# A gated mix of linear attention and a squared-ReLU layer: all products as two streams of 64-row halves, in one fixed order for all engines

## The chip, the cores and the metric

The kernel runs on one core of a Trainium2 chip. The metric is the device time of one execution in microseconds (us). The kernel before took 447.13 us, the median of three runs (446.76 to 447.21).

The engines are named as in the profile: PE (TensorE, matmuls), PEld (its weight loads), DVE (VectorE), ACT (ScalarE), POOL (GpSimd), SP (SyncE, which issues most DMAs). SBUF and the accumulators in PSUM have 128 partitions, here called rows where a matmul contracts over them. PSUM is used in eight banks of 128 x 512 float32.

## The reference

All tensors are float32; S = 2048 tokens, D = 448, F = 1792, 16 heads of 28.

```
x = A_x
g = sigmoid((x * gate_w).sum(-1))
q, k, v = split(x @ wqkv)                      # per head
phi = lambda t: where(t > 0, t + 1, exp(t)) + 1e-6
pq, pk = phi(q), phi(k)
kv = einsum("bhsd,bhse->bhde", pk, v);  z = pk.sum over s
o = (pq @ kv) / (pq . z + 1e-6)
a = o @ wo
h = relu(x @ w1 + b1) ** 2
b = h @ w2 + b2
return g * a + (1 - g) * b
```

## The kernel before

**Precision.** Each float32 operand is split into a rounded high part and the rest (`split_hi`, `split_lo`), and a product is computed as three: high times high, high times low, low times high. Over the D = 448 input columns that is 3 x 448 = 1344 rows of contraction. The host pads x and the weights to four chunks of 128 rows, the last of which holds columns 384 to 447 twice; `split_last` writes high and low parts crosswise into its two halves, so that two matmuls do the work of three there. A product over D thus takes 11 matmuls (`terms_x`, `terms_w`, `up_chunk`).

**Tiling.** Tokens go in four blocks `b` of 512, each of four tiles of 128. The squared-ReLU layer goes over F in 14 slices `f` of 128: `up(b, f)` makes `h_ps` (128 x 512, 11 matmuls), `hidden` applies bias, ReLU and square on ACT and splits the result into `hh` and `hl` on DVE, and `down(b, f)` adds its product with `w2` into the four banks `o_ps` (12 matmuls of 448 columns). The seven first slices of all blocks come first, then the seven others; `half_done` and `finish` empty `o_ps`.

**Attention** is worked in between. In the first phase `keys(t)` makes `k_ps` (11 matmuls) and phi of it, and `gram(b, c)` sums products of keys and tokens in `g_ps`. Then `key_sums` (`z_ps`), `kv_product` (`kv_ps`) and `m_product` (`m_ps`) fold v and wo into one matrix `m_s`, which POOL's DMAs put together. In the second phase `queries(b, c)` (`q_ps`; 11 matmuls, 7 for the fourth block, whose halves are swapped by DMAs and added), `denominators(b)` (`d_ps`), `scaled` and `attention(b, i)` (`a_ps`, 11 matmuls) follow.

**Order and buffers.** Two loops over `b` and `f` write the steps in the order up, down, attention work, loads and splits; work that empties a bank is put off by one step (`todo`, `run_todo`). The framework places the instructions of each engine from that. Banks come from three pools: four for `o_ps`, two for `h_ps`, two for the rest. Most SBUF buffers are 14 rotating slots of one tag (`slot`); the queries' operands are 15 of another (`late`).

Of the kernel before, what the change touches and what calls it, by code (L numbers as in the profile page):

```python
# [1 line left out]

# [12 lines left out]
DH = D // H  # L15
# [13 lines left out]

@with_exitstack  # L30
def gated_mix_kernel(ctx: ExitStack, tc: tile.TileContext, xt, xn, wk, wq, wv, wo, w1a, w1b, w2, b1, b2, hmask,
                     kvmask, halves, out):
    nc = tc.nc
    act, dve, pool, pe, sp = nc.scalar, nc.vector, nc.gpsimd, nc.tensor, nc.sync
# [10 lines left out]
    NSLOT, NLATE = 14, 15  # L45

    def slot(shape, dt, name):
        return work.tile(shape, dt, name=name, tag="s", bufs=NSLOT)
# [25 lines left out]
    def products(out_ps, terms):  # L74
        n = len(terms)
        for i, (a, b) in enumerate(terms):
            pe.matmul(out_ps, a, b, start=(i == 0), stop=(i == n - 1))  # L77


    def terms_x(xh, xl, cols, w, wcols, c):  # L80
        if c == 3:
            return [(xh[:, 3, cols], w[:, 3, wcols]), (xl[:, 3, cols], w[:, 3, wcols])]
        return [(xh[:, c, cols], w[:, c, wcols]), (xh[:, c, cols], w[:, 4 + c, wcols]),
                (xl[:, c, cols], w[:, c, wcols])]

    def terms_w(xh, xl, w, wcols):
        t = []
        for c in range(3):
            t += [(w[:, c, wcols], xh[:, c]), (w[:, c, wcols], xl[:, c]), (w[:, 4 + c, wcols], xh[:, c])]
        return t + [(w[:, 3, wcols], xh[:, 3]), (w[:, 3, wcols], xl[:, 3])]  # L90

# [5 lines left out]
    def load_x(b, c, a=0, z=TB):  # L97
        if a == 0:
            x_raw[b, c] = slot([P, TB], F, f"xr{b}_{c}")
        load(x_raw[b, c][:, a:z], xt[b, c][:, a:z])  # L100

    def split_x(b, c, a=0, z=TB):
        if c == 0 and a == 0:
            xs[b] = (keep.tile([P, 4, TB], R, name=f"xh{b}", tag="xh", bufs=2),
                     keep.tile([P, 4, TB], R, name=f"xl{b}", tag="xl", bufs=2))
        (xh, xl), r = xs[b], x_raw[b, c]
# [6 lines left out]
    def split_w(w, c, src, hi_eng, lo_eng):  # L113
        split_hi(hi_eng, w[:, c], src)
        if c < 3:
            split_lo(lo_eng, w[:, 4 + c], src, w[:, c])
        else:
            split_lo(lo_eng, w[64:, 3], src[64:], w[64:, 3])
# [4 lines left out]
    def load_w1(h, g, c):  # L123
        w1_raw[h, g, c] = slot([P, (TB, 3 * P)[g]], F, f"w1r{h}{g}{c}")
        load(w1_raw[h, g, c], (w1a, w1b)[g][h, c])

    def split_w1(h, g, c, hi_eng=act):
        if c == 0:
            w = keep.tile([P, (3648, 2716)[g]], R, name=f"w1_{h}{g}", tag=f"w1{g}", bufs=1)

            n, a = (4, 3)[g], ((4, 20), (4, 16))[g][h]
            w = w[:, a:a + 900 * n].rearrange("p (i k) -> p i k", k=900)[:, :, :7 * P]
            w1_s[h, g] = w.rearrange("p i (c j) -> p c i j", c=7)
        split_w(w1_s[h, g], c, w1_raw.pop((h, g, c)).rearrange("p (i k) -> p i k", k=P), hi_eng, dve)


    W2_AT = [56, 48, 40, 28, 20, 12, 4, 18, 14, 17, 15, 16, 2, 10]
    w2_s, w2_raw = {}, {}

    def load_w2(f):  # L140
        w2_raw[f] = slot([P, D], F, f"w2r{f}")
        load(w2_raw[f], w2[f])

    def split_w2(f):
        w = keep.tile([P, 960], R, name=f"w2_{f}", tag="w2", bufs=NH)
        w = w[:, W2_AT[f]:W2_AT[f] + 2 * D]
        w2_s[f] = w.rearrange("p (s n) -> p s n", s=2)
        split_hi(act, w2_s[f][:, 0], w2_raw[f])
        split_lo(dve, w2_s[f][:, 1], w2_raw.pop(f), w2_s[f][:, 0])
# [3 lines left out]
    def load_xn(t):  # L153
        xn_raw[t] = slot([P, D], F, f"xnr{t}")
        load(xn_raw[t], xn[t])
# [3 lines left out]
    def load_wk(c):  # L159
        wk_raw[c] = slot([P, D + 2], F, f"wkr{c}")  # L160
        load(wk_raw[c], wk[c])

    warm = keep.tile([P, 400], mybir.dt.bfloat16, name="warm")[:, :256]
    dve.memset(warm, 0.0)
# [4 lines left out]
    side = rest.tile([P, 56], F, name="side")[:, :2]  # L172
# [11 lines left out]
    b1_s = keep.tile([P, NF], F, name="b1_s")  # L184
    half = keep.tile([P, 2], F, name="half")
    ones = keep.tile([P, 2], F, name="ones")
    logit = keep.tile([P, NT], F, name="logit")
    gate = keep.tile([P, 2, NT], F, name="gate")
    zc = keep.tile([P, 4], F, name="zc")
# [14 lines left out]
    tmp_p = phase1.enter_context(tc.tile_pool(name="tmp_p", bufs=1, side="right"))  # L204

# [3 lines left out]
    def up_chunk(ps, b, f, c):  # L209
        h, fl = divmod(f, NH)  # L210
        g, i = divmod(fl, 4)
        w, cols = w1_s[h, g], i
        xh, xl = xs[b]
        if c < 3:
            terms = [(w[:, c, cols], xh[:, c]), (w[:, c, cols], xl[:, c]), (w[:, 4 + c, cols], xh[:, c])]
        else:
            terms = [(w[:, 3, cols], xh[:, 3]), (w[:, 3, cols], xl[:, 3])]
        for n, (a, m) in enumerate(terms):
            pe.matmul(ps, a, m, start=(c == 0 and n == 0), stop=(c == 3 and n == 1))  # L219

    def hidden(ps, b, f):
        r = slot([P, TB], F, f"hr{b}_{f}")
        act.activation(r, ps, AF.Relu, bias=b1_s[:, f:f + 1])  # L223
        act.activation(r, r, AF.Square)  # L224
        h = slot([P, TB], R, f"hh{b}_{f}")
        lo = slot([P, TB], R, f"hl{b}_{f}")
        split_hi(dve, h, r)
        split_lo(dve, lo, r, h)
        hs[f] = (h, lo)

    def up(b, f):
        ps = mm_p.tile([P, 512], F, name=f"h_ps{b}_{f}", tag="mm")
        for c in range(4):
            up_chunk(ps, b, f, c)
        hidden(ps, b, f)

    o_ps = {}

    def down(b, f, tiles=range(4)):
        h, lo = hs[f]  # L240
        w = w2_s[f]
        for i in tiles:
            if f % NH == 0:
                o_ps[i] = acc_p.tile([P, 512], F, name=f"o_ps{b}_{f}_{i}", tag="acc")
            cols = slice(i * P, (i + 1) * P)
            terms = [(h[:, cols], w[:, 0]), (h[:, cols], w[:, 1]), (lo[:, cols], w[:, 0])]
            for n, (a, m) in enumerate(terms):
                pe.matmul(o_ps[i][:, :D], a, m, start=(f % NH == 0 and n == 0),  # L248
                          stop=(f % NH == NH - 1 and n == 2))

    def half_done(b):
        for i in range(4):
            dve.tensor_tensor(part[4 * b + i], o_ps[i][:, :D], b2_s, op=ALU.add)

    def finish(b, i):
        t = 4 * b + i
        u = slot([P, D], F, f"out{t}")
        dve.scalar_tensor_tensor(u, o_ps[i][:, :D], gate[:, 1, t:t + 1], part[t], op0=ALU.mult, op1=ALU.add)
        sp.dma_start(out=out[t * P:(t + 1) * P, :], in_=u)
# [3 lines left out]
    gsum = []  # L263
# [5 lines left out]

    def keys(t):  # L270
        b, i = divmod(t, 4)
        ps = ms_p.tile([P, 512], F, name=f"k_ps{t}", tag="ms")
        products(ps[:, :D + 2], [term for c in range(4)
                                 for term in terms_x(*xs[b], slice(i * P, (i + 1) * P), wk_s, slice(0, D + 2), c)])
        e = slot([P, D], F, f"e{t}")
        r = slot([P, D], F, f"r{t}")
        p = r
        ph = tmp_p.tile([P, D], R, name=f"ph{t}", tag="ph", bufs=4)
        pl = tmp_p.tile([P, D], R, name=f"pl{t}", tag="pl", bufs=4)

        if t == 0:
            pool.memset(tmp_p.tile([P, 48], F, name="off"), 0.0)

        def after():
            phi(ps[:, :D], e, r, p)
            dve.tensor_copy(logit[:, t:t + 1], ps[:, D:D + 1])
            split_hi(act, ph, p)
            split_lo(dve, pl, p, ph)
            if t == 0:
                pool.tensor_copy(ksum, p)  # L290
            else:
                pool.tensor_tensor(ksum, ksum, p, op=ALU.add)  # L292
            nh = tmp.tile([P, 512], R, name=f"nh{t}", tag="nh", bufs=4)
            nl = tmp.tile([P, 384], R, name=f"nl{t}", tag="nl", bufs=4)
            raw = xn_raw.pop(t)
            split_hi(act, nh[:, :D], raw)
            split_lo(pool, nl, raw[:, :384], nh[:, :384])
            split_lo(pool, nh[:, D:], raw[:, 384:], nh[:, 384:D])
            pend[t] = (ph, pl, nh, nl)
        return [after]  # L300

    def gram(b, c):
        ps = ms_p.tile([P, 512], F, name=f"g_ps{b}_{c}", tag="ms")
# [5 lines left out]
        products(ps[:, :D], terms)  # L309

        def after():
            if b == 0:
                gsum.append(tmp.tile([P, D], F, name=f"gsum{c}"))
                act.copy(gsum[c], ps[:, :D])
            else:
                dve.tensor_tensor(gsum[c], ps[:, :D], gsum[c], op=ALU.add)
        return [after]

    wq_s = keep.tile([P, 7, TB], R, name="wq_s")
# [438 lines left out]
```

## Time and profile before

| | |
|---|---|
| median of 3 runs | 447.13 us |
| the profiled execution: span from first to last instruction | 445.7 us |
| matmuls in the program / in the trace | 2034 / 2054 |
| DMA: moved, mean rate | 28.77 MB, 65 GB/s |

The program's 20 float32 matmuls (`kv_ps`, `z_ps`) stand in the trace as two each, hence 2054. A matmul row gives the time from its start to the modelled end of its result, so successive rows overlap; the pace of the matmuls is the difference of their starts, or the length of a group divided by its count. Idle time stands in front of the instruction that had to wait, with what ended it.

```profile
DMA packets 18315, 28.77 MB, mean 65 GB/s; under 512 B 2880, under 2 KB 12784, under 8 KB 18288
```

### The profile page before, as it was taken

To read this page: it belongs to the slowest core of one execution; us is meant where nothing else is said; L and a number is where in the kernel's file an instruction comes from. 1 tells how busy PE (TensorE), PEld (TensorE's weight loads), DVE (VectorE), ACT (ScalarE), POOL (GpSimd) and SP (SyncE) were. 2 spreads that over 40 slices of the span, in tenths; PEclk is the share of its full clock that TensorE was granted. 3 is DMA by queue.
4 is the path that set the end of the run, shared out by engine and by line. 5 is a ranking of instruction groups with operands and counts; after the bars stand their busy time and mean duration, and the time that the engine had idled before them with its cause. 6 is when DMAs were issued, how large, how long until landed. Compare 5 with 4: busy or idle time off the path is not lost.

```text
span 445.7 us, 5473 instructions
## 1 busy us (share of the span) xinstructions
PE 438.7 (98%) x2054; PEld 381.9 (86%) x2054; DVE 269.1 (60%) x452; ACT 172.2 (39%) x298; POOL 58.0 (13%) x76
## 2 busy tenths in 40 slices
PE   8999999999999999999999989999999999999996
PEld 6798898889888888888988868888888898888885
DVE  5867536552587426672466678788455974549423
ACT  5855335331355113542344235245232443234221
POOL 0143123210252005420002420000000000000000
PEclk9999999999999999999999999999999999999999
DMA  8462202020131201332245310050100501002002
GB/s 268 149 201 68 88 0 69 24 65 22 47 116 31 66 21 43 91 100 63 71 124 146 71 38 24 1 171 6 26 0 0 179 0 26 0 0 84 1 1 82
DMA packets 18315, 28.77 MB, mean 65 GB/s; under 512 B 2880, under 2 KB 12784, under 8 KB 18288
## 3 DMA queue, kind: packets, MB, share of 16 engines
q1 hardware_dynamic: 17072, 26.81, 19.6%
q0 software_dynamic: 1216, 1.61, 1.7%
q8 instruction: 16, 0.26, 0.3%
q14 instruction: 11, 0.09, 0.1%
HBM read 22.09 MB, written 3.67 MB: 58 GB/s over the span
## 4 chain that ended last, share of the span: by engine, by line
PE 93%; DVE 3%; ACT 2%; issue 1%; DMA 1%; SPq 0%; DVEq 0%; ACTq 0%
PE h_ps L219 30%; PE o_ps L248 30%; PE q_ps L77 8%; PE a_ps L77 8%; PE g_ps L77 8%; PE k_ps L77 7%; DMA xr<-in_xt 1%; PE kv_ps L370 1%; ACT hr L223 1%; PE m_ps L77 1%; ACT hr L224 0%; DVE r L268 0%; DVE r L267 0%; PE d_ps L77 0%; DVE hh L62 0%
## 5 line engine op out<-in xcount | busy, mean ns | idle before, releaser
L219 PE MATMUL h_ps<-xh,w 128*128 128x512 f32 x392 | 128.8, 397 | 0.3 <-ACT xh L58 0.2
L248 PE MATMUL o_ps<-w,hh 128*128 128x448 f32 x448 | 126.9, 366 | 0.5 <-DVE hh L62 0.5
L248 PEld LDWEIGHTS o_ps<-w,hh 128*128 128x128 f32 x448 | 84.1, 188 | 10.8 <-DVE hh L62 1.2
L219 PE MATMUL h_ps<-xl,w 128*128 128x512 f32 x224 | 88.4, 395 | 0.0
L219 PEld LDWEIGHTS h_ps<-xh,w 128*128 128x128 f32 x392 | 73.9, 189 | 16.9 <-ACT xh L58 0.7
L248 PE MATMUL o_ps<-w,hl 128*128 128x448 f32 x224 | 80.1, 365 | 0.0
L223 ACT ACTIVATE hr<-h_ps,b_s 128x512 f32<-128x512 f32 x56 | 38.3, 683 | 102.9 <-PE h_ps L219 101.6
L62 DVE CAST hh<-hr 128x512 fp32r<-128x512 f32 x56 | 25.4, 454 | 43.6 <-ACT hr L224 43.2
L219 PEld LDWEIGHTS h_ps<-xl,w 128*128 128x128 f32 x224 | 42.4, 189 | 8.8
L248 PEld LDWEIGHTS o_ps<-w,hl 128*128 128x128 f32 x224 | 42.3, 189 | 3.6 <-DVE hl L65 0.2
L65 DVE TENSOR_TENSOR hl<-hr,hh 128x512 fp32r<-128x512 f32 x56 | 41.9, 748 | 1.9
L224 ACT ACTIVATE hr<-hr 128x512 f32<-128x512 f32 x56 | 35.3, 630 | 1.3
L77 PE MATMUL k_ps<-wk_s,xh 128*128 128x450 f32 x112 | 33.6, 367 | 0.0
L77 PE MATMUL q_ps<-xh,wq_s 128*128 128x512 f32 x100 | 33.2, 391 | 0.0
L77 PE MATMUL a_ps<-m_s,qh 128*128 128x448 f32 x112 | 32.7, 366 | 0.0
L65 POOL TENSOR_TENSOR nl<-xnr,nh 128x384 fp32r<-128x384 f32 x16 | 17.2, 1078 | 96.5 <-ACT nh L58 96.5
L487 DVE SCALAR_TENSOR_TENSOR part<-part,gate,u 128x448 f32<-128x448 f32 x16 | 10.9, 684 | 26.7 <-ACT u L486 26.7
L292 POOL TENSOR_TENSOR ksum<-ksum,r 128x448 f32<-128x448 f32 x15 | 19.3, 1284 | 52.3 <-DVE r L268 52.3
L486 ACT ACTIVATE u<-a_ps,gate 128x448 f32<-128x448 f32 x16 | 10.2, 635 | 38.1 <-PE a_ps L77 38.1
L267 DVE TENSOR_SCALAR r<-k_ps 128x448 f32<-128x448 f32 x16 | 10.0, 624 | 23.7 <-ACT e L266 23.6
L77 PE MATMUL g_ps<-pl,nh 128*128 128x448 f32 x64 | 23.3, 365 | 0.3 <-DVE pl L65 0.3
L77 PE MATMUL q_ps<-xl,wq_s 128*128 128x512 f32 x60 | 23.6, 393 | 0.0
(104 smaller groups left out, 562.5 us busy)
## 6 DMA issues: line engine op xcount, KB each, us to landing
xr<-in_xt SPq DMA_DIRECT2D x27, 256.0 KB, 3.1
xnr<-in_xn SPq DMA_DIRECT2D x16, 224.0 KB, 2.5
out<-out SPq DMA_DIRECT2D x16, 224.0 KB, 2.0
w2r<-in_w SPq DMA_DIRECT2D x14, 224.0 KB, 2.5
w1r<-in_w1a SPq DMA_DIRECT2D x8, 256.0 KB, 2.8
w1r<-in_w1b SPq DMA_DIRECT2D x8, 192.0 KB, 3.4
m_s<-m POOLq DMA_DIRECT2D x12, 112.0 KB, 2.8
wqr<-in_wq SPq DMA_DIRECT2D x4, 256.0 KB, 2.8
```

The lines of the kernel that those rows point to most:

```text
L62: eng.tensor_copy(hi, src)
L65: eng.tensor_tensor(lo, src, f32(hi), op=ALU.subtract)
L77: pe.matmul(out_ps, a, b, start=(i == 0), stop=(i == n - 1))
L219: pe.matmul(ps, a, m, start=(c == 0 and n == 0), stop=(c == 3 and n == 1))
L223: act.activation(r, ps, AF.Relu, bias=b1_s[:, f:f + 1])
L224: act.activation(r, r, AF.Square)
L248: pe.matmul(o_ps[i][:, :D], a, m, start=(f % NH == 0 and n == 0), stop=(f % NH == NH - 1 and n == 2))
L267: dve.tensor_scalar(r, ps, 0.0, 1e-6, op0=ALU.max, op1=ALU.add)
L292: pool.tensor_tensor(ksum, ksum, p, op=ALU.add)
L370: pe.matmul(kv_ps[:JE, js], wv_s[c][:, js], gsum[c][:, js], start=(c == 0), stop=(c == 3))
L486: act.activation(u, ps[:, :D], AF.Copy, scale=gate[:, 0, t:t + 1])
L487: dve.scalar_tensor_tensor(part[t], part[t], gate[:, 1, t:t + 1], u, op0=ALU.mult, op1=ALU.add)
```

## The change

**Halves.** Every matmul over 128 rows becomes two over 64: one on rows 0 to 63 (`LO`), one on rows 64 to 127 (`UP`), each with all its output columns into a whole bank. The last chunk needs no crossing trick any more: one half holds one term, the other half two, so a product over D is 21 halves instead of 11 matmuls of 128 rows. Only the last 12 matmuls of the program and the 18 warm-up ones stay whole. The program has 3938 matmuls instead of 2034.

```diff
+LO, UP = slice(0, 64), slice(64, P)
...
+def halves(terms):
+    return [[(a[r], m[r], None) for a, m in terms] for r in (LO, UP)]
+
+
+def last_halves(terms, swapped=False):
+
+    low, high = halves(terms)
+    return (low[:1], high[::-1]) if swapped else (low, high[1:])
```

**Two streams and a bank that is passed on.** The `LO` halves form one stream, the `UP` halves another. At a time a bank belongs to one of them; when its halves are done, the other stream takes the bank, and its first matmul there waits for the last one of the former stream.

```diff
+    def emit(self, j, s):
...
+        a, m, where = j.left[s].pop(0)
+        if b.of not in (None, s):
+            wait = tc.keep_in_program_order(pe.nop())
+            tc.add_manual_dep(wait.ins, b.last, AFTER, reason="the bank goes to the other half of the rows")
+        b.seen += 1 + j.whole
+        ins = pe.matmul(b.ps[where or b.whole], real(a), real(m), start=b.seen == 1 + j.whole, stop=b.seen == b.total)
+        tc.keep_in_program_order(ins)
```

In the built program the waiting no-op is merged into the matmul behind it: 322 matmuls wait for an earlier matmul, where 21 did before.

**One list.** `Flow.run` plays the whole program through with a table of durations and writes the instructions of all engines in the order that comes out (`keep_in_program_order`); each stream may choose among the next 12 products the one that can start first, and each engine among the next 60 queued operations.

```diff
+    def product(self, s):
+
+        if self.current[s] is not None:
+            return self.stream[s], self.current[s]
+        best = None
+        jobs, at = self.jobs, self.at
+        for k in range(at[s], min(at[s] + AHEAD, len(jobs[s]))):
+            j = jobs[s][k][1]
...
+            r = self.ready(j, s)
+            if r is not None and (best is None or r < best[0] - 1e-9):
+                best = r, j
...
     for b in range(1, NB):
         for f in range(NH):
+            jobs = up(b, f)
+            jobs += down(b, f - 1) if f else down(b - 1, NH - 1)
...
+    steps.append(Step(down(order[-1], NF - 1, whole=True)))
+    flow.run(steps, {"acc": 4, "mm": 2, "ms": 2})
```

**Fixed slots and layout.** Buffers are fixed tiles that an operation takes when it is written (15 slots, 14 for the queries' operands, two for `m`). The host orders the heads so that the swap of the fourth query block exchanges rows 0 to 63 with 64 to 127 in two DMAs instead of eight per block; `m_s` is put together by 32 DMAs of POOL instead of 20. `finish` adds the attention part first or last, whichever is ready later.

```diff
-            for p in range(0, P, 16):
-                load(r[p:p + 16], v[p ^ 16:(p ^ 16) + 16])
...
+            for p in (0, 64):
+                load(r[p:p + 64], v[p ^ 64:(p ^ 64) + 64])
...
-    head = 4 * (p // 32) + p % 16 // 4
...
+    head = p % 64 // 4
```

**The order on TensorE, at three places.** In the middle of block 3 (`h_ps3_2` is the product of its slice 2, `o_ps3_0_1` the bank of its second tile, `hh` and `hl` or the slots their operands, `k_ps` the keys) the program before had, one product after the other:

```order
L219 MATMUL h_ps3_2_1639<-xl3_1322,w1_00_169 128x512
L248 MATMUL o_ps3_0_0_1591<-w2_1_248,hh3_1_1587 128x448 [waits DVE_49]
L248 MATMUL o_ps3_0_0_1591<-w2_1_248,hh3_1_1587 128x448
L248 MATMUL o_ps3_0_0_1591<-w2_1_248,hl3_1_1588 128x448 [waits DVE_49]
L248 MATMUL o_ps3_0_1_1595<-w2_1_248,hh3_1_1587 128x448 x2
L248 MATMUL o_ps3_0_1_1595<-w2_1_248,hl3_1_1588 128x448
L248 MATMUL o_ps3_0_2_1599<-w2_1_248,hh3_1_1587 128x448 x2
L248 MATMUL o_ps3_0_2_1599<-w2_1_248,hl3_1_1588 128x448
```

Now the same work stands like this; the rows are halves, `LO` and `UP` in turn:

```order
L310 MATMUL o_ps3_0_0_2478<-w2_all_82,slot12_2444 128x448 [waits DVE_49]
L310 MATMUL h_ps3_1_2419<-x2_78,w10_80 128x512
L310 MATMUL o_ps3_0_1_2490<-w2_all_82,slot13_2430 128x448
L310 MATMUL h_ps3_1_2419<-x2_78,w10_80 128x512
L310 MATMUL o_ps3_0_1_2490<-w2_all_82,slot13_2430 128x448
L310 MATMUL o_ps3_0_1_2490<-w2_all_82,slot12_2444 128x448
L310 MATMUL o_ps3_0_0_2478<-w2_all_82,slot13_2430 128x448 [waits PE_49]
L310 MATMUL o_ps3_0_2_2499<-w2_all_82,slot13_2430 128x448
L310 MATMUL o_ps3_0_0_2478<-w2_all_82,slot13_2430 128x448
L310 MATMUL o_ps3_0_2_2499<-w2_all_82,slot13_2430 128x448
L310 MATMUL o_ps3_0_0_2478<-w2_all_82,slot12_2444 128x448
L310 MATMUL o_ps3_0_2_2499<-w2_all_82,slot12_2444 128x448
```

While `LO` works on the third tile, `UP` takes over the first, six halves after `LO` left it; `[waits PE_49]` marks the handover.

At the start, behind the first four `h_ps` products, the program before went on with `down(0, 0)`:

```order
L219 MATMUL h_ps0_3_164<-xl0_166,w1_00_169 128x512
L248 MATMUL o_ps0_0_0_280<-w2_0_245,hh0_0_234 128x448 [waits DVE_49]
L248 MATMUL o_ps0_0_0_280<-w2_0_245,hh0_0_234 128x448
L248 MATMUL o_ps0_0_1_284<-w2_0_245,hh0_0_234 128x448 x2
L248 MATMUL o_ps0_0_0_280<-w2_0_245,hl0_0_235 128x448 [waits DVE_49]
```

Now the first keys stand there:

```order
L310 MATMUL h_ps0_1_210<-x0_76,w10_80 128x512
L310 MATMUL k_ps0_351<-wkm_83,x0_76 128x450 [waits Activation_49]
L310 MATMUL k_ps0_351<-wkm_83,x0_76 128x450 [waits DVE_49]
L310 MATMUL k_ps0_351<-wkm_83,x1_77 128x450
L310 MATMUL k_ps0_351<-wkm_83,x0_76 128x450
L310 MATMUL k_ps0_351<-wkm_83,x0_76 128x450 [waits DVE_49]
L310 MATMUL k_ps0_351<-wkm_83,x1_77 128x450
```

The keys moved ahead of the first `down`; these halves are all of one stream, and the second stream's keys follow behind them.

In the second phase, at the denominators of block 2, the program before had:

```order
L248 MATMUL o_ps1_7_3_3114<-w2_13_2252,hl1_13_3416 128x448
L77 MATMUL d_ps2_3496<-dh2_3449,hm_135 128x512 [waits Activation_49]
L77 MATMUL d_ps2_3496<-dl2_3450,hm_135 128x512 [waits DVE_49]
L219 MATMUL h_ps2_8_3506<-xh2_3143,w1_10_1814 128x512
L219 MATMUL h_ps2_8_3506<-xl2_3144,w1_10_1814 128x512
```

and now (`x1` and `x0` hold the high and low parts of x):

```order
L310 MATMUL h_ps2_8_5531<-x1_77,w10_80 128x512
L310 MATMUL h_ps2_9_5547<-x1_77,w10_80 128x512 x2
L310 MATMUL h_ps2_9_5547<-x0_76,w10_80 128x512
L310 MATMUL h_ps2_9_5547<-x1_77,w10_80 128x512
L310 MATMUL h_ps2_9_5547<-x0_76,w10_80 128x512
L310 MATMUL h_ps2_9_5547<-x1_77,w10_80 128x512
L310 MATMUL d_ps2_5577<-slot0_5558,hm_105 128x512 [waits Activation_49]
L310 MATMUL h_ps2_8_5531<-x1_77,w10_80 128x512 [waits PE_49]
```

Six halves of `h_ps2_9` stand behind one another in the `UP` stream, with none of `LO` between them: this is one of the runs of three or more halves of one stream. There are five such runs of `LO`, with 33 halves, and seven of `UP`, with 30; all other halves alternate singly or in twos. Each stream has 916.6 thousand columns in all.

More of the change, by code (lines that the diff above doesn't have):

```diff
@@ L72, in split_last @@
         split_lo(dve, crossed, src, straight)
[L74 to L90, printed above, removed]
+    steps = []
     x_raw, xs = {}, {}
@@ L227, in hidden, with up_bank @@
         split_hi(dve, h, r)
         split_lo(dve, lo, r, h)
-        hs[f] = (h, lo)
-    def up(b, f):
[L232 to L241, printed above, removed]
+        close(r)
+        hs[b, f] = (h, lo)
+    ups, o_ps, a_banks = {}, {}, {}
+    def up_bank(b, f, pool=mm_p, tag="mm"):
+        bank = ups[b, f] = Bank(pool, f"h_ps{b}_{f}", tag, 21)
+        bank.done = lambda: hidden(bank.ps, b, f)
+        return bank
@@ L245, in down @@
[L245 to L255, printed above, removed]
-        t = 4 * b + i
-        u = slot([P, D], F, f"out{t}")
-        dve.scalar_tensor_tensor(u, o_ps[i][:, :D], gate[:, 1, t:t + 1], part[t], op0=ALU.mult, op1=ALU.add)
-        sp.dma_start(out=out[t * P:(t + 1) * P, :], in_=u)
+                o_ps[i] = Bank(acc_p, f"o_ps{b}_{f}_{i}", "acc", 6 * NH, D)
@@ new lines, in down, with half_done, store @@
+                o_ps[i].done = partial(half_done if f < NH else finish, b, i, o_ps[i])
+            terms = partial(down_terms, b, f, i)
+            split = (lambda t=terms: [[(*x, None) for x in t()], []]) if whole else (lambda t=terms: halves(t()))
+            jobs.append(Job(o_ps[i], split, C448, [("h", b, f), ("w2", f)], whole=whole))
+        return jobs
+    def half_done(b, i, bank):
+        dve.tensor_tensor(part[4 * b + i], bank.ps[:, :D], b2_s, op=ALU.add)
+    def store(t, ps, old):
+        u = slot(D)
+        dve.scalar_tensor_tensor(u, ps, gate[:, 1, t:t + 1], old, op0=ALU.mult, op1=ALU.add)
+        sp.dma_start(out=out[t * P:(t + 1) * P, :], in_=u)
+        close(u)
```

1087 lines of the change are left out of this document (704 added, 383 removed).

## The prediction

> **What bounds the kernel now.** I begin with the head of the profile page.
>
> ```profile
> span 445.7 us, 5473 instructions
> PE 438.7 (98%) x2054; PEld 381.9 (86%) x2054; DVE 269.1 (60%) x452; ACT 172.2 (39%) x298; POOL 58.0 (13%) x76
> PEclk9999999999999999999999999999999999999999
> PE 93%; DVE 3%; ACT 2%; issue 1%; DMA 1%; SPq 0%; DVEq 0%; ACTq 0%
> ```
>
> TensorE has a matmul under way in 98% of the span, its granted clock is full in all 40 slices, and 93% of the chain that ended last is TensorE. Time can only come from fewer or faster matmuls, or from the moments at which TensorE stands. I read the pace of the matmuls from the chain of waits in order of time (start, duration, piece).
>
> ```profile
> 5.31 9.89 PE h_ps L219 x38
> ...
> 166.34 2.43 PE o_ps L248 x12
> 168.77 2.25 PE k_ps L77 x11
> 171.02 2.56 PE h_ps L219 x11
> ...
> 183.27 2.27 PE k_ps L77 x11
> ...
> 205.12 2.41 PE g_ps L77 x12
> 207.53 0.79 PE z_ps L349 x8
> ...
> 223.97 3.15 PE kv_ps L370 x32
> ...
> 232.16 2.52 PE q_ps L77 x11
> ...
> 319.16 2.26 PE a_ps L77 x11
> ...
> 436.99 5.16 PE o_ps L248 x24
> 442.18 0.68 DVE out L258
> ```
>
> One matmul takes 2.56/11 = 232.7 ns in `h_ps`, 229.1 in `q_ps` (both 512 columns), 2.43/12 = 202.5 in `o_ps`, 200.8 in `g_ps`, 204.5 in `k_ps`, 205.5 in `a_ps` (448 or 450 columns). The code has 616 `h_ps`, 160 `q_ps`, 672 `o_ps`, 176 each of `g_ps`, `k_ps` and `a_ps`, and 20 of `m_ps` and `d_ps`. At these paces they take 143.3 + 36.7 + 136.1 + 35.3 + 36.0 + 36.2 + 4.3 us; with 0.79 for `z_ps` and 3.15 for `kv_ps` that is **431.8 us**. TensorE worked from 5.31 to about 442.18, which is 436.9 us: **5.1 us** were lost to waiting or to slower pieces. What it waited for is in the view of TensorE's waits (total us, times, longest):
>
> ```profile
> PE d_ps L77 <- ACT dh L58: 1.3, 1, 1.3
> PE o_ps L248 <- DVE hh L62: 0.5, 1, 0.5
> PE g_ps L77 <- DVE pl L65: 0.3, 1, 0.3
> PE h_ps L219 <- ACT xh L58: 0.2, 1, 0.2
> ```
>
> So the named waits are few, 2.3 us in all. The rest of the 5.1 us is at the start, where 38 matmuls took 9.89 us for 38 x 0.2327 = 8.84, and in small gaps.
>
> **The change, part by part.** (1) *Fewer columns through the array.* A product over 448 input columns, three terms of the precision split each, has 3 x 448 = 1344 rows of contraction, 10.5 times 128. Before, it is 11 matmuls, the last of them padded by crossing. Afterwards it is 21 halves of 64 rows, two streams of which are meant to run side by side: 10.5 pairs. If a pair takes as long as one full matmul does now, each such product saves half a matmul: 56 `h_ps` x 0.5 x 232.7 = 6.5 us, 12 of the `q_ps` x 0.5 x 229.1 = 1.4, 16 `k_ps` x 0.5 x 204.5 = 1.6, 16 `a_ps` x 0.5 x 205.5 = 1.6. `o_ps`, `g_ps`, `m_ps`, `d_ps` and four `q_ps` have no padding and save nothing. **Sum: 11.2 us off, 420.6 us of TensorE work.**
>
> (2) *The pace of a pair.* No row of this profile has two matmuls on different rows at once, so I bound it. What the trace does show is this (timeline, two stretches; PEld is the weight load):
>
> ```profile
> 208.15 0.19 PEld L219 LDWEIGHTS h_ps<-xh,w 128*128 128x128 f32 x1
> 208.26 0.19 PEld L219 LDWEIGHTS h_ps<-xl,w 128*128 128x128 f32 x1
> ...
> 300.25 0.39 PE L219 MATMUL h_ps<-xl,w 128*128 128x512 f32 x1
> 300.25 0.19 PEld L219 LDWEIGHTS h_ps<-xh,w 128*128 128x128 f32 x1
> 300.48 0.40 PE L219 MATMUL h_ps<-xh,w 128*128 128x512 f32 x1
> ```
>
> Each load starts with the matmul before it and is hidden by it. Two loads can follow each other in 208.26 - 208.15 = 0.11 us, which is half of the 0.23 us between the matmuls. From above, then: if nothing overlaps, a pair costs two matmuls; if only the loads of the two streams stand in one line, a pair costs at least 2 x 0.11 = 220 ns. That is still under the 229 to 233 ns of the 512-column pairs but 17 ns above the 203 ns of the 448-column ones. From below: the paces of the 448-column groups differ by 205.5 - 200.8 = 5 ns among themselves, and I allow 3 ns of gain on each of some 1190 such pairs, 3.6 us. I take **no change of pace**: the nearest row is the full matmul, whose columns, weight columns and clock are those of each half. Break-even stands at 11.2 us / 1960 pairs = 5.7 ns per pair, so this value decides nearly everything.
>
> The Trainium skill speaks against the change at one place: "TensorE: Matmul & The Clock Gate", section "Measured speedup vs the span model", adds about 4 ns for each further tile that runs in the array. By that, 1960 pairs would take 7.8 us more and the sum below would be 445.6 us. No run here shows it; I leave it out because a stream that follows on without a gap should not pay a start more than once.
>
> (3) *Handing a bank over.* Each bank is begun by one stream and finished by the other, so 322 matmuls now carry a wait for an earlier matmul, where 21 did. Behind such a wait stands everything in TensorE's queue, the other stream included. The nearest rows are the `k_ps` groups at 168.77 (no such wait) and 183.27 (the first of its matmuls waits for an earlier matmul): 2.25 and 2.27 us, so a wait whose cause lies a dozen matmuls back costs at most 0.02 us. In the order shown above the cause lies six or seven halves back. A bound from above: a matmul of 448 columns lives longer than its pace, and a wait that exposes the difference costs 366 - 203 = 163 ns, 52 us in all.
>
> ```profile
> L248 PE MATMUL o_ps<-w,hh 128*128 128x448 f32 x448 | 126.9, 366 | 0.5 <-DVE hh L62 0.5
> L404 POOL DMA_DIRECT2D m_s<-m x12 | 6.4, 542 | 2.2 <-DVE m L65 2.1 <-issue 0.2
> ```
>
> I take 0, by the `k_ps` rows. Break-even lies at about 30 ns per handover.
>
> (4) *Halves that run alone.* The order holds runs of three or more halves of one stream: 33 of the lower rows in five runs, 30 of the upper rows in seven. One of each run belongs to the alternation, so the other stream is idle beside (33 - 5) or (30 - 7) halves, about 25 x 0.21 = 5.3 us. These take the place of the waits of before (5.1 us); I add 1.0 us for moments at which both stand, since the start waits for the splits of x and w1, as it does now. Term: 5.3 + 1.0 - 5.1 = **+1.2 us**. Bounds: 0 to 12 us in place of the 6.3, the upper end if each run's cause is as late again.
>
> (5) *The rest I cost at nothing, with its cover.* VectorE and ScalarE do nearly the same work in another order. Their fullest stretch is in this table (us, length, then busy time and count of PE, PEld, DVE, ACT, POOL):
>
> ```profile
> 234.00:270.00 36.00, 34.66 (x156) 29.00 (x156) 25.27 (x43) 13.68 (x25) 10.57 (x20) 1.00 0.34 81
> 270.00:300.00 30.00, 30.00 (x141) 26.21 (x140) 24.02 (x40) 11.74 (x20) 0.00 (x0) 1.00 0.19 62
> ```
>
> VectorE is at 80% there, so it stays under a TensorE that is 2.6% shorter; without that cover a late `hh` costs what it costs now, 0.5 us a time. The 12 more DMAs that POOL issues for `m_s` take 12 x 0.542 = 6.5 us on a POOL that is busy 10.6 of 36 us there; they land before `a_ps` needs them as long as queries fill TensorE, otherwise up to 6.5 us appear once. The swap of the fourth query block issues 2 DMAs in place of 8, off the path. The tail (the last 12 matmuls on all rows, `out`, its DMA) is the same: 445.7 - 442.18 = 3.5 us.
>
> **The sum.** Against the profiled execution: 445.7 - 11.2 + 1.2 = 435.7 us of span. The median of the runs is 447.13, 1.4 us above the span, so the time is 437.1; the bounds of (4) lean upwards, and I say **437.8 us**, 2.1% faster.
>
> **The rivals.** *Weight loads in one line.* If both streams' loads share one path, every 448-column pair takes 220 ns: 1190 x 17 ns = 20 us, so 437.8 + 20 = **458 us**, slower. It decides from 5.7 ns per pair on. For it: two loads never stand closer than 0.11 us in this profile. Against it: here all loads use all rows, so nothing shows that loads on different rows must queue. The skill has both sides: "TensorE: Matmul & The Clock Gate", section "LDWEIGHTS (loading the stationary operand)", says that a load takes its time by columns whatever the rows, 107 ns for 128, and the trace's 0.11 us agrees; "TensorEngine Tiling (Array Packing)", section "Key Properties", says that different tiles load and multiply in parallel, which no run here shows.
>
> *Handovers that show.* If each of the 322 waits costs 40 ns (a quarter of the 163), 13 us come back: **451 us**; at 20 to 30 ns the result is 444 to 447. For it: the queue is in order, so a wait of one stream stops both. Against: the `k_ps` rows.
>
> *No overlap at all.* The change would not do what it says: 2 x 420.6 plus 16 is about **857 us**. Against it speaks only that rows that are not shared need not wait for each other.
>
> *Better than the sum.* Pairs 3 ns faster, or no halves alone: **432 us** or less.
>
> **Chances.** Forecast 0.66 (432.5 to 443), handovers or other partial loss 0.14 (443 to 452), loads in one line 0.12, no overlap 0.02, better 0.06. The range 432.5 to 452 holds the first two, 0.80, and reaches from the better end of the unknown pace to a handover of 40 ns. A measurement of this kernel can tell about 0.2% (0.9 us) from no change. Of the partial losses I put 0.05 below 446.2, 0.03 within 0.2% and 0.06 above: faster 0.66 + 0.06 + 0.05 = 0.77, same 0.03, slower 0.06 + 0.12 + 0.02 = 0.20.
>
> **What would show it.** Right: 21 halves of an `h_ps` paired with others at 230 to 235 ns per pair, `o_ps` pairs at 200 to 206, two matmuls of about 0.37 to 0.40 us starting at nearly the same time; weight loads of both streams overlapping; few waits of TensorE on itself. Wrong on (2): `o_ps` pairs at 215 to 225 ns while `h_ps` pairs keep 232. Wrong on (3): gaps of TensorE in front of halves that wait for a matmul. Wrong on (4): long waits for VectorE or ScalarE with one stream silent, above all before 20 us and between 215 and 270 us.

## The result, and the profile after

| | before | after |
|---|---|---|
| median of the runs | 446.98 us (446.76 to 447.21, 4 runs) | 441.45 us (440.80 to 443.03, 4 runs) |
| the profiled execution: its time, its span | 447.13, 445.7 us | 441.48, 439.7 us |
| start of the first to end of the last matmul of the products | 5.31 to 442.14 us | 5.38 to 436.07 us |

The ratio is **0.988** (95% interval 0.986 to 0.990): 1.2% faster, where 2.1% was forecast. The head of the page of the changed kernel (span; busy time, share and count by engine; clock by slices; the chain that ended last, by engine) answers to the one shown first in the prediction.

```profile
span 439.7 us, 9349 instructions
PE 433.8 (99%) x3978; PEld 413.3 (94%) x3978; DVE 268.5 (61%) x454; ACT 172.2 (39%) x298; POOL 67.5 (15%) x91
PEclk9999999999999999999999999999999999999999
PE 91%; DVE 5%; ACT 1%; DMA 1%; issue 0%; SPq 0%; DVEq 0%; ACTq 0%
```

Nearly twice as many matmuls fill a shorter span at the same clock. The timeline of the middle of the program (start, duration, piece; PEld is the weight load) shows that the two streams do run beside each other. At 299 us both streams multiply 512 columns:

```profile
299.29 0.39 PE L310 MATMUL h_ps<-x,w 64*128 64x512 f32 x1
299.30 0.18 PEld L310 LDWEIGHTS h_ps<-x,w 64*128 64x128 f32 x1
299.31 0.39 PE L310 MATMUL q_ps<-x,wq_s 64*128 64x512 f32 x1
299.31 0.18 PEld L310 LDWEIGHTS q_ps<-x,wq_s 64*128 64x128 f32 x1
299.53 0.39 PE L310 MATMUL h_ps<-x,w 64*128 64x512 f32 x1
...
299.54 0.39 PE L310 MATMUL q_ps<-x,wq_s 64*128 64x512 f32 x1
```

Each stream starts a half every 0.23 to 0.24 us, the pace of a whole matmul before, and the loads start 0.01 us apart. Before, two loads of 128 weight columns never stood closer than 0.108 us (those of `kv_ps`, with 112 columns, 0.10 us, so the prediction's 0.11 is not quite the least). At 189 us both work on 448 or 450 columns:

```profile
189.01 0.36 PE L310 MATMUL k_ps<-wkm,x 64*128 64x450 f32 x1
189.08 0.36 PE L310 MATMUL o_ps<-w_all,slot 64*128 64x448 f32 x1
189.21 0.36 PE L310 MATMUL k_ps<-wkm,x 64*128 64x450 f32 x1
189.28 0.36 PE L310 MATMUL o_ps<-w_all,slot 64*128 64x448 f32 x1
```

Here the step is 0.20 us in each stream. Over the whole trace, the median time from one half to the next of the same stream is 232 ns in `h_ps`, 200 in `o_ps` and 205 in `k_ps`; before, from one matmul to the next, it was 232, 203 and 205 ns. In `o_ps` the steps fall into two groups, near 200 and near 206 ns, and their mean without the gaps is 202 ns now and 203.4 before.

**What was lost.** TensorE's waits behind the warm-up (total us, times, longest) are now misleading:

```profile
PE o_ps L310 <- DVE slot L209: 0.4, 1, 0.4
PE h_ps L310 <- ACT x L209: 0.3, 1, 0.3
PE d_ps L310 <- DVE slot L209: 0.2, 1, 0.2
```

0.9 us in all, less than the 2.3 before. But such a view sees TensorE idle only when both streams stand; a stream that stands beside a busy one leaves PE busy. So I took from the trace, for each stream, the time from every matmul's start to the next one's, less a fixed pace (231.7 ns for 512 columns, 204.5 for 450, 203.5 for 448). What is left over is called **lost** below. By these paces the work is 432.7 us with 11 matmuls (or 22 halves) per product over `D`, and 421.5 us with 21 halves. Before lost 4.15 us; after lost 9.1 us in the lower stream and 9.2 in the upper. Lost is a net figure: steps that are shorter than the fixed pace are set off against the standing.

The loss is in a few places. In the table by stretches (start and end, length, then busy time and count of PE, PEld, DVE, ACT, POOL; PEclk, DMA share, GB/s), the count of matmuls tells it, not the busy time:

```profile
16.00:19.00 3.00, 3.00 (x16) 2.42 (x14) 1.32 (x3) 3.00 (x6) 0.00 (x0) 1.00 0.65 232
60.00:63.00 3.00, 3.00 (x33) 2.92 (x31) 0.81 (x2) 0.00 (x0) 0.00 (x0) 1.00 0.52 164
191.20:194.20 3.00, 2.94 (x21) 2.07 (x20) 2.60 (x5) 2.24 (x4) 1.64 (x2) 1.00 0.00 1
300.00:303.00 3.00, 3.00 (x30) 2.84 (x28) 3.00 (x5) 1.32 (x2) 0.00 (x0) 1.00 0.00 0
```

The count holds every half that is under way in the stretch. Two full streams show 30 to 33 in 3 us; from 16 to 19 us there are 16, from 191.2 on 21, with PE "busy" for all or nearly all of it. The timeline of the start, TensorE alone (start, duration, piece):

```profile
13.61 3.15 PE L310 MATMUL h_ps<-x,w 64*128 64x512 f32 x19
16.58 3.65 PE L310 MATMUL k_ps<-wkm,x 64*128 64x450 f32 x20
```

And one row of the same timeline at 191 us:

```profile
191.25 2.98 PE L310 MATMUL h_ps<-x,w 64*128 64x512 f32 x15
```

From 15.3 us on the lower stream waits, 1.0 us longer than a step, for ScalarE before its first `k_ps` half; then the upper stream, which holds no bank and finds none free, stands 2.5 us until the lower one is through with `k_ps` and hands the bank over. From 192.0 us on the same: the upper stream stands 1.5 us while the lower one runs its halves of `h_ps3_5` alone. The next largest is at 276.8 us (1.0 us), ahead of the first `a_ps`, whose first half waits for VectorE; the chain of waits there is VectorE's own work:

```profile
265.30 7.39 DVE slot L209 x12
272.69 2.47 DVE q L209 x4
...
276.37 1.61 DVE slot L209 x3
278.02 0.47 PE a_ps L310
```

The rest is in pieces of at most 0.7 us, the largest of them at 342 and 396 us.

### The profile page after: what moved, and what is told of

It reads as the page before. It is cut to its first block, busy times and chain, and to the rows that moved or that the text cites. A ratio compares the mean times of both kernels' runs of the same rounds, so it can differ in the third digit from the quotient of the medians.

```text
span 439.7 us, 9349 instructions
## 1 busy us (share of the span) xinstructions
PE 433.8 (99%) x3978; PEld 413.3 (94%) x3978; DVE 268.5 (61%) x454; ACT 172.2 (39%) x298; POOL 67.5 (15%) x91
## 4 chain that ended last, share of the span: by engine, by line
PE 91%; DVE 5%; ACT 1%; DMA 1%; issue 0%; SPq 0%; DVEq 0%; ACTq 0%
PE h_ps L310 31%; PE o_ps L310 28%; PE a_ps L310 8%; PE g_ps L310 8%; PE k_ps L310 7%; PE q_ps L310 7%; DVE slot L209 4%; ACT slot L209 1%; PE kv_ps L310 1%; DMA slot<-in_xt 1%; DVE q L209 1%; PE m_ps L310 1%; PE d_ps L310 0%; ACT x L209 0%; PE z_ps L310 0%
## 5 line engine op out<-in xcount | busy, mean ns | idle before, releaser
L310 PE MATMUL h_ps<-x,w 64*128 64x512 f32 x1176 | 257.3, 394 | 0.4 <-ACT x L209 0.3
L310 PE MATMUL o_ps<-w_all,slot 64*128 64x448 f32 (+1 forms) x1332 | 240.5, 363 | 0.4 <-DVE slot L209 0.4
L310 PEld LDWEIGHTS o_ps<-w_all,slot 64*128 64x128 f32 (+1 forms) x1332 | 205.7, 184 | 6.5 <-DVE slot L209 1.8
L310 PEld LDWEIGHTS h_ps<-x,w 64*128 64x128 f32 x1176 | 193.6, 185 | 7.5 <-ACT x L209 0.8
L310 PE MATMUL q_ps<-x,wq_s 64*128 64x512 f32 x308 | 74.3, 393 | 0.0
L310 PE MATMUL k_ps<-wkm,x 64*128 64x450 f32 x336 | 66.3, 364 | 0.0
L209 DVE TENSOR_TENSOR slot<-slot,slot 128x512 fp32r<-128x512 f32 (+2 forms) x85 | 61.3, 733 | 4.4 <-DMA slot<-slot 1.7
L310 PE MATMUL a_ps<-wkm,q 64*128 64x448 f32 x336 | 62.2, 361 | 0.1
L310 PEld LDWEIGHTS k_ps<-wkm,x 64*128 64x128 f32 x336 | 57.0, 185 | 1.4 <-ACT slot L209 0.2
L310 PEld LDWEIGHTS q_ps<-x,wq_s 64*128 64x128 f32 x308 | 55.1, 184 | 1.5 <-DVE slot L209 0.3
## 6 DMA issues: line engine op xcount, KB each, us to landing
slot<-in_w1b SPq DMA_DIRECT2D x8, 192.0 KB, 4.0
```

Source lines behind the costliest of these rows:

```text
L209: op = Op(lambda: method(*[real(x) for x in args], **{k: real(x) for k, x in kwargs.items()}), self.cost(name, kind, out, [x for x in aps ...
L310: ins = pe.matmul(b.ps[where or b.whole], real(a), real(m), start=b.seen == 1 + j.whole, stop=b.seen == b.total)
```

## The experiments

Each edit is shown against the changed kernel. "First to last" is from the first to the last matmul of the products, "lost" is as above (the mean of both streams), and the span is that of the profiled execution. Each ratio is to runs of the kernel before that were measured beside it (medians 446.98 for after, 447.15 for e1, e2, e4 and e5, 446.94 for e3, e6 and e7).

| kernel | median us | ratio to before, 95% | span | first to last | lost |
|---|---|---|---|---|---|
| before | 446.98 | | 445.7 | 436.8 | 4.2 |
| after | 441.45 | 0.988 (0.986 to 0.990) | 439.7 | 430.7 | 9.2 |
| e1_one_stream | 443.42 | 0.991 (0.990 to 0.993) | 441.7 | 432.4 | -0.3 |
| e2_22_halves | 453.07 | 1.014 (1.012 to 1.016) | 451.0 | 441.9 | 9.2 |
| e4_no_margin | 464.63 | 1.040 (1.038 to 1.041) | 462.8 | 453.3 | 31.8 |
| e5_ahead_20 | 438.09 | 0.980 (0.978 to 0.982) | 436.3 | 427.4 | 5.9 |
| e3_ahead_10 | 449.56 | 1.006 (1.004 to 1.008) | 451.1 | 442.0 | 20.4 |
| e6_one_pool | 435.74 | 0.974 (0.971 to 0.977) | 434.2 | 425.1 | 3.5 |
| e7_one_stream_ahead_6 | 449.02 | 1.004 (1.002 to 1.006) | 447.5 | 438.5 | 5.8 |

**e1: the list without the halves.** Whole matmuls over all 128 rows in one stream, with the new list, slots and layout; the padding of before (11 matmuls) is back, its low-times-low term too.

```diff
-        self.whole, self.left, self.taken, self.ready = whole, None, [False, False], [None, None]
+        self.whole, self.left, self.taken, self.ready = whole, None, [False, True], [None, None]
...
-    return [[(a[r], m[r], None) for a, m in terms] for r in (LO, UP)]
+    return [[(a, m, None) for a, m in terms], []]
...
-    return (low[:1], high[::-1]) if swapped else (low, high[1:])
+    return low, high
...
+        self.jobs[1] = []
...
-        bank = ups[b, f] = Bank(pool, f"h_ps{b}_{f}", tag, 21)
+        bank = ups[b, f] = Bank(pool, f"h_ps{b}_{f}", tag, 11)
```

> The new list, slots and layout with whole 128-row matmuls in one stream: 11 per product again, no bank is passed on. Theory idle (a pair of halves costs what one full matmul costs; what is missing from the 11.2 us is time in which one stream has nothing to do): TensorE works 11.2 us more than in the changed kernel, and the one stream is idle only some 4 us instead of 9, so about 446 to 447.5 us, the same as before; the list alone gains nothing. Rival handover (the missing 5 us are paid at waits for the other stream's matmuls): without handovers the new list would show a better order by itself, 442 us or less. Rival order (the gain came from the order and the slots, not from the halves): 441 to 442 us.

Measured: 443.42 us, faster than the theory said by some 3 us, and 1.4 us short of the two rivals, to which it is nearer. I had taken the list for neutral; alone it is worth 3.7 us against the kernel before, measured beside it (447.15). That is two thirds of the 5.5 us that the whole change gains. Four neighbouring pieces of its chain of waits (start, duration, piece):

```profile
84.31 2.24 PE k_ps L310 x11
86.55 2.50 PE h_ps L310 x11
89.05 2.43 PE o_ps L310 x12
91.48 2.41 PE g_ps L310 x12
```

Piece follows on piece without a gap, and `k_ps`, `h_ps` and `o_ps` together take 7.17 us where the prediction's rows at 166 us have 7.24. Its named waits of TensorE behind the warm-up are two (total us, times, longest):

```profile
PE h_ps L310 <- ACT x L209: 1.0, 1, 1.0
PE o_ps L310 <- DVE slot L209: 0.9, 1, 0.9
```

With them, the whole still loses nothing against the fixed paces (-0.3 us), because two things cancel. Steps that come late by more than 0.03 us add up to 2.0 us here and to 4.8 before; and the other steps are shorter, by some 1.6 us on balance (`a_ps` 200.1 ns in place of 204.0, `o_ps` 201.8 in place of 203.4, means without the gaps). The changed kernel has the shorter steps too (`a_ps` 200.9 to 201.7, `o_ps` 202.0 to 202.2), so they belong to the list or its layout and not to the halves. The halves alone, with the list already there, bring only 443.42 - 441.45 = 2.0 us (1.8 if each is compared with the kernel before measured beside it): 11.2 us of columns saved, against 9.2 + 0.3 = 9.5 us that one stream does not lose.

**e2: the padding back.** Two streams as in the changed kernel, but 22 halves per product, which adds the half that holds only low times low.

```diff
-    return (low[:1], high[::-1]) if swapped else (low, high[1:])
+    return (low, high[::-1]) if swapped else (low, high)
...
-        bank = ups[b, f] = Bank(pool, f"h_ps{b}_{f}", tag, 21)
+        bank = ups[b, f] = Bank(pool, f"h_ps{b}_{f}", tag, 22)
```

(and 22 for 21 in the banks of `k_ps`, `q_ps` and `a_ps`.)

> Two streams as in the changed kernel, but each product over D keeps its 22nd half (a low-times-low term that the changed kernel leaves out; it changes the sums only in the last bits), so the padding of before is back. Theory idle: 100 more halves, 50 pairs, that is 42 x 232 ns (h_ps, q_ps... 56 + 12 products of 512 columns and 32 of 448) = 68 x 0.5 x 0.232 + 32 x 0.5 x 0.204 = 11.2 us more: 452 to 453 us, slower than the kernel before, since the idle of two streams stays. Rival handover: also 452 to 453. Rival pace (halves of a pair slow each other): the difference to the changed kernel would be more than 11.2 us, 12 or more.

Measured: 453.07 us, 11.6 us above the changed kernel, with the same loss of 9.2 us; from the first to the last matmul the difference is 441.9 - 430.7 = 11.2 us. The saving of half a matmul per product is real and has the size of step (1). It also shows that two streams with all of the old work would be 6 us slower than before.

**e4: no margin at handovers.** The list plans a handover 0.4 us after the other stream's last half; now 0.

```diff
-LATE, SIGNAL, LANDING, HANDED = 0.25, 0.08, 1.9, 0.4
+LATE, SIGNAL, LANDING, HANDED = 0.25, 0.08, 1.9, 0.0
```

> The list is made as if a bank could be passed on at once (HANDED 0 in place of 0.4): 72 handovers have their cause only three halves back instead of 3. Its own plan leaves each stream idle about 5 us longer than that of the changed kernel. Theory idle, with a handover that costs only when its cause is nearer than about 0.4 us: 446 us by the plan, plus some 0.15 to 0.25 us for each of the about 80 close ones (both streams stop), 12 to 20 us: 458 to 466 us. Rival handover (each of the handovers costs alike, some 10 to 15 ns, whatever the distance): about 446 us.

Measured: 464.63 us, as expected by the view that a handover costs something only where its cause is near. The timeline at one of them, in which the upper half of `o_ps` takes over a bank whose last lower half started at 105.33 us, three halves back:

```profile
105.53 0.36 PE L310 MATMUL g_ps<-p,nh 64*128 64x448 f32 x1
105.75 0.47 PE L310 MATMUL o_ps<-w_all,slot 64*128 64x448 f32 x1
105.75 0.47 PE L310 MATMUL g_ps<-p,nh 64*128 64x448 f32 x1
106.06 0.36 PE L310 MATMUL o_ps<-w_all,slot 64*128 64x448 f32 x1
106.06 0.36 PE L310 MATMUL g_ps<-p,nl 64*128 64x448 f32 x1
```

The upper stream's half before had started at 105.21 us, so this one comes 0.33 us late, and the next start follows after 0.31 us in place of 0.20, in both streams. A wait for another engine acts in the same way. At 95.00 us the `o_ps` half waits for VectorE (in brackets the idle time before and what ended it); the `k_ps` half behind it in the queue waits for nothing and was due at 94.56:

```profile
94.15 0.35 PE L310 MATMUL o_ps<-w_all,slot 64*128 64x448 f32 x1
94.35 0.37 PE L310 MATMUL k_ps<-wkm,x 64*128 64x450 f32 x1
95.00 0.47 PE L310 MATMUL o_ps<-w_all,slot 64*128 64x448 f32 x1 [0.28 <-DVE slot L209]
95.00 0.47 PE L310 MATMUL k_ps<-wkm,x 64*128 64x450 f32 x1
```

A half that waits at the head of the queue thus holds the other stream as well. In this kernel the 71 handovers whose cause lies 3 halves back (a few in the changed kernel) start 0.10 us late on average. In the changed kernel those with a cause 7 to 9 halves back, the largest group (101 of 310), start within 0.004 us of the pace. Not all of the 23 us are handovers: the edit changes the list elsewhere (its plan stands 5 us longer), and for 6.8 us TensorE's granted clock was half (PEclk, the third figure from the end), which is worth at most 3.4 us:

```profile
24.80:31.60 6.80, 5.28 (x22) 4.02 (x24) 6.71 (x13) 3.33 (x7) 1.11 (x3) 0.50 0.01 4
```

What it settles is that the 0.4 us of margin buys step (3). In the changed kernel only two handovers cost much, those at 16 and 192 us (2.5 and 1.5 us in the upper stream); their causes lie two halves and one half back, since the upper stream had nothing else to start.

**e3, e5, e6: the loss itself.** If the 9 us stand because a stream finds no product to start or no free bank, then a shorter choice must lose more, and a longer one with more banks to choose from less. `AHEAD` is the number of products among which a stream chooses (12), and `PATIENCE` is by how many us the operations that come in with a step stand back in rank. e3:

```diff
-AHEAD, PATIENCE, SPARE = 12, 5.0, 3
+AHEAD, PATIENCE, SPARE = 10, 5.0, 3
```

> The changed kernel with a choice among the next 10 products for each stream instead of 12; same halves, 487 handovers instead of 474. Theory idle: the work is the same 421.5 us, the list's own plan leaves each stream idle 6.8 us longer than that of the changed kernel, so 447 to 449 us, no longer faster than the kernel before. Rival (the list's order and slots gain of themselves, one stream or two, and the halves give the rest): a slightly shorter choice changes little, 441 to 443 us.

e5, in which the second keys also take their bank from the other pool:

```diff
-AHEAD, PATIENCE, SPARE = 12, 5.0, 3
+AHEAD, PATIENCE, SPARE = 20, 9.0, 3
...
-        bank = key_banks[t] = Bank(ms_p, f"k_ps{t}", "ms", 21, D + 2)
+        bank = key_banks[t] = Bank(*((mm_p, f"k_ps{t}", "mm") if t == 1 else (ms_p, f"k_ps{t}", "ms")), 21, D + 2)
```

> Same work, same halves and about as many handovers (461 in place of 474); each stream may choose among 20 products in place of 12, steps enter with another patience (9 in place of 5), and the second keys take a bank of the h_ps pool, so that the upper rows need not wait at the start. Its own plan leaves each stream idle 4.4 us less than that of the changed kernel (5.6 in place of 10.0). Theory idle: 4.4 us faster than the changed kernel, 436 to 438 us. Rival handover: no change, 441 us.

e6, in which the two pools of two banks are one pool of four (every `"ms"` becomes `"mm"`):

```diff
-AHEAD, PATIENCE, SPARE = 12, 5.0, 3
+AHEAD, PATIENCE, SPARE = 24, 7.0, 3
...
-    mm_p = ctx.enter_context(tc.tile_pool(name="mm_p", bufs=2, space=PSUM))
-    ms_p = ctx.enter_context(tc.tile_pool(name="ms_p", bufs=2, space=PSUM))
+    mm_p = ctx.enter_context(tc.tile_pool(name="mm_p", bufs=4, space=PSUM))
+    ms_p = mm_p
...
-    flow.run(steps, {"acc": 4, "mm": 2, "ms": 2})
+    flow.run(steps, {"acc": 4, "mm": 4})
```

> The four banks of the h_ps and of the other products become one pool, so that a stream that has to wait for the other's bank can open any free one; choice among 24 products, patience 7. Same work and halves. Theory idle: the plan leaves each stream idle 5.9 us less than that of the changed kernel and 1.4 us less than the version with a choice among 20, so 435.5 to 437.5 us. Rival (below some 437 us something else ends last, the data for the start or VectorE between 240 and 280 us): no better than the version with 20, 438 us.

Measured: 449.56 and 438.09 (both just above what was expected) and **435.74 us**, with 20.4, 5.9 and 3.5 us lost. The profiled execution of e3 took 452.96 us: for 6.8 us, from 358.4 us on, its granted clock was half, behind a stretch in which the streams stood; that is up to 3.4 of its 20.4 us. All its other runs have a mean clock of 0.991 to 0.996 too, so up to some 2 us of its median are the clock. In after, e5 and e6 the clock is full between 8 us and the last matmul. The work and the halves are the same in all four kernels; from after to e6, the loss falls by 5.6 us and the time by 5.7. e6 is faster than both kernels of the case. Its table by stretches, at two of the places shown above:

```profile
16.00:19.00 3.00, 3.00 (x26) 2.66 (x26) 1.12 (x2) 2.80 (x6) 0.00 (x0) 1.00 0.97 356
...
191.20:194.20 3.00, 3.00 (x31) 2.95 (x29) 3.00 (x5) 2.17 (x4) 1.55 (x1) 1.00 0.78 229
```

and its timeline of the start, TensorE alone:

```profile
13.80 2.69 PE L310 MATMUL h_ps<-x,w 64*128 64x512 f32 x15
16.30 4.94 PE L310 MATMUL k_ps<-wkm,x 64*128 64x450 f32 x42
```

26 halves instead of 16, and 31 instead of 21: at the start the two streams now run the halves of two different `k_ps` banks, 42 in 4.9 us, and neither has to wait for the other's bank. How much of e6 is the one pool and how much the longer choice and the other patience was not tried apart.

**e7: the choice with one stream.** The edits of e1, and a choice of 6 instead of 12. Is it two streams that need the choice, or any list of this kind?

```diff
-AHEAD, PATIENCE, SPARE = 12, 5.0, 3
+AHEAD, PATIENCE, SPARE = 6, 5.0, 3
```

> One stream of whole matmuls in the new list, but with a choice among the next 6 products instead of 12. Theory: two streams need a longer choice than one, because a product occupies its bank until both streams are through; with one stream the plan grows by only 5.5 us from 12 to 6 (it grows by 19 us with two), so 447 to 449 us. Rival (the length of the choice matters alike for both): 455 us or more.

Measured: 449.02 us, 5.6 above e1. Seven of the twelve runs have a mean clock of 0.996 (in the profiled one it is half for 3.4 us, worth up to 1.7); the five at full clock took 447.65 to 448.27 us, as the theory said, 4.2 to 4.9 above e1. The view of waits names most of it (total us, times, longest):

```profile
PE o_ps L310 <- DVE slot L209: 4.1, 5, 1.1
```

One stream pays for a short choice too, but it lost nothing at 12, where two streams lost 9.2 us. With whole matmuls the wait is visible in this view; with two streams 9 us stand behind three rows of 0.9 in all.

## Why the prediction was right, and where it was not

(1) **Fewer columns**: right. Forecast -11.2 us; by the paces used here 432.7 - 421.5 = 11.2, and putting the padding back costs 11.6 (e2).

(2) **The pace of a pair**: right. The marks were 230 to 235 ns for `h_ps` and 200 to 206 for `o_ps`; measured 232, and 200 in the median and 202 in the mean. "Weight loads in one line" and "no overlap" fall with the loads 0.01 us apart. The Trainium skill's rule in "TensorE: Matmul & The Clock Gate", section "Measured speedup vs the span model", of some 4 ns for each further tile, shows only between two halves that start together, which lie 2 to 5 ns apart in the trace (19.139 and 19.143 us); it does not add to the pace, since streams that follow on keep that of one matmul. The Trainium skill's page "TensorEngine Tiling (Array Packing)", section "Key Properties", by which different tiles load and multiply in parallel, agrees with this trace.

(3) **Handovers**: right that they cost about nothing here, but the row behind the zero could not show it. The `k_ps` group at 183.27 us waits for a matmul 58 matmuls back, not a dozen, so it says nothing of a cause six or seven halves back; as far as the zero rests on that row, it came true by luck. That such handovers are free is shown by the trace after; e4 brings the causes nearer, and then they cost.

(4) **Halves that run alone**: the term that was mis-sized. I forecast 6.3 us lost in place of the 5.1 of before, +1.2. By one measure for both kernels it is 9.2 in place of 4.15, **+5.0**. The sum then reads -11.2 + 5.0 = -6.2 us, and the trace has 436.8 - 430.7 = 6.1 from the first to the last matmul; the medians differ by 5.5, since the time outside the span also grew, from 447.13 - 445.7 = 1.4 to 441.48 - 439.7 = 1.8 us.

What was mis-sized is not what the step counted. Beside the five runs of the lower rows the upper stream came 4.75 us late, beside the seven runs of the upper rows the lower stream 3.2 us: 4.0 us on average, where 5.3 was forecast. (An order does not show how long a stream stands beside a run: the twelve lower halves from 16.6 us on cost 2.5 us because the other stream had no bank, and three of the twelve runs cost nothing.) The remaining 5.2 us (net of shorter steps) stand where the step allowed 1.0, "for moments at which both stand". Sorted by what the late half itself waits for in the program, steps late by more than 0.03 us add up as follows:

| the late half waits for | lower stream, us | upper stream, us |
|---|---|---|
| a matmul of the other stream | 0.7 | 4.9 |
| VectorE or ScalarE | 5.3 | 1.3 |
| nothing | 4.2 | 4.0 |

Of the last row 0.4 and 0.8 us fall before 7 us, where the granted clock is not yet full. The others stand in the queue behind a half of the other stream that waits (0.5 us at 342.3), or follow a stop, after which the next start comes about 0.1 us late (0.31 in place of 0.20 us, as in e4). The prediction's sign for this, long waits for VectorE or ScalarE, came true, but not only at the places named ("above all before 20 us and between 215 and 270 us"): before 20 us the two streams lost 2.2 and 3.7 us, but 192 us, 276.8 us and everything behind 340 us, some 4 us in the lower stream, were not foreseen.

The bounds of that step, 0 to 12 us, did hold the value. What they hid is that two effects cancel in it: by e1 the list alone makes up for the old loss of 4.15 (less standing and shorter steps) and gains 3.7 us, and the two streams bring in a new one that is 9.5 above e1's. The step had both effects, 5.1 us off and 6.3 on, and it was the second that it made too small. The prediction weighed the list and the halves as one, and so could not see that the halves by themselves gain 2 us.

(5) **The rest at nothing**: the tail is the same (436.07 to the end of the span is 3.6 us, 3.5 before). The last rows of the timeline show the closing matmuls on all rows and the issues of the output:

```profile
434.71 1.36 PE L310 MATMUL o_ps<-w_all,slot 128*128 128x448 f32 x6
...
435.02 2.14 SPq L209 DMA_DIRECT2D out<-slot  x4
```

POOL's additional DMAs stay hidden: the last one for `m_s` is issued at 253 us, none takes over 4.0 us to land, and the first `a_ps` half at 278 us waits for VectorE alone, whose row of 7.39 us is shown above. The cover of VectorE and ScalarE did not hold as forecast: late halves that wait for them cost the lower stream 5.3 us, against 3.4 us for TensorE before by the same count. This belongs to the term of step (4).

One thing stays open: why the pieces of e1, and of all kernels with the list, are up to some 1% (in `a_ps` 2%) shorter than the same matmuls of before. No run separates the new layout from the new order.

A further remark on where the loss sits: `Flow.run` plays the program through with fixed durations before anything runs. By its own arithmetic, which is no measurement, 428.3 us pass between the starts of the first and the last product matmul of the changed kernel, with some 8 us of standing in each stream; on the chip it is 430.3 us (5.38 to 435.7). Most of the standing is planned into the list, which is why a few settings of the planner move it.

## What to carry to other kernels

Two streams of 64-row halves run at full pace beside each other and save exactly the padding that they remove; what they cost is standing, because every accumulator is held until both streams are through with it and a wait of one stream stops both. They need a longer choice of work than one stream to stay full (at a choice of 12 two lost 9.2 us and one lost nothing), and more freedom in the banks probably helps (one pool of four in place of two of two, with a choice of 24: 435.74 us in place of 441.45; the pool was not tried alone). Judge such a kernel by the number of matmuls started per microsecond, not by the busy share of TensorE or its list of waits, which stay clean while half of the array stands. And before crediting a change that brings a new schedule along with a new shape, run the new schedule with the old shape.

## What the runs showed of the hardware

Weight loads on different rows start 0.01 us apart and last 184 to 185 ns each for 64 rows, against 188 to 189 ns on all rows before: half the rows do not load faster, but both halves load at once. The groups of loads (line, engine, shapes, count, then busy us and mean ns, idle before and what ended it), the largest of before and the two largest of after, show it:

```profile
L248 PEld LDWEIGHTS o_ps<-w,hh 128*128 128x128 f32 x448 | 84.1, 188 | 10.8 <-DVE hh L62 1.2
...
L310 PEld LDWEIGHTS o_ps<-w_all,slot 64*128 64x128 f32 (+1 forms) x1332 | 205.7, 184 | 6.5 <-DVE slot L209 1.8
L310 PEld LDWEIGHTS h_ps<-x,w 64*128 64x128 f32 x1176 | 193.6, 185 | 7.5 <-ACT x L209 0.8
```

A half that waits for the other stream's half starts at the soonest some 0.057 us after the modelled end of that one, and one wait stops both streams (e4, from 94.35 to 95.00 us, for VectorE).

A half that only stands behind halves of its own stream does not hold the other one. In the list of the changed kernel the first half of `a_ps8` (lower rows) comes behind four halves of `o_ps` (upper rows), which start at 411.30, 411.50, 411.70 and 411.90 us; on the chip it starts at 411.35, ahead of three of them:

```profile
411.12 0.39 PE L310 MATMUL h_ps<-x,w 64*128 64x512 f32 x1
411.30 0.36 PE L310 MATMUL o_ps<-w_all,slot 64*128 64x448 f32 x1
411.35 0.42 PE L310 MATMUL a_ps<-wkm,q 64*128 64x448 f32 x1
411.50 0.36 PE L310 MATMUL o_ps<-w_all,slot 64*128 64x448 f32 x1
```

So a run of one stream in the order need not leave the other one idle.
